# Regrouping small matmuls by TensorE mode and reordering two DMA queues in a fused attention and MLP kernel

## The chip, the cores and the metric

The kernel runs on one core of a Trainium2 chip. The metric is the device time of one execution in microseconds. Besides the time of whole runs I use a finer measure, because differences of 0.2 us are at stake in 290: inside a trace, the time from the start of one matmul to that of another.

## The reference, cut to what matters

```python
kv  = np.einsum('bhsd,bhse->bhde', k, v)          # 8 batches, 8 heads, 576 rows, 64 columns
out = np.einsum('bhsd,bhde->bhse', q, kv)         # linear attention, no softmax
x   = out / rms(out) * g_norm                     # per head
xn  = (x - mean) / sqrt(var + 1e-6) * g_ln        # per row of 512
y   = x + relu(xn @ w_ch1) @ w_ch2                # 512 -> 2048 -> 512
```

## The kernel before

Work is cut into tiles of 128 rows. A batch has 576 rows: four full tiles and a remainder of 64 rows, and two batches' remainders share a tile ("remainder 1" holds those of batches 0 and 1, and so on). For a full tile, `o` is four matmuls of the full form, 128 rows by 128 columns; `kv` of a batch and the remainder's `o` use only 64 of TensorE's columns at a time, because their outputs go to one half of the PSUM partitions each:

```python
def kv_of(b):                                     # 40 matmuls, 128 rows x 64 columns
    kv_ps = ps_m.tile([128, HP, D], f32, tag="misc", name="kv_ps")
    ...
                nc.tensor.matmul(kv_ps[hh * D:hh * D + D, hp, :],
                                 lhsT=k_in[b % NB][:, h, j, :], rhs=v_in[b % NB][:, h, j, :], ...)
    nc.scalar.copy(kvp[:D, :, :D], kv_ps[:D])
    nc.scalar.copy(kvp[D:, :, D:], kv_ps[D:])
```

TensorE's stream is the two large products (`mm1`, line 413, and `mm2`, line 429 of this kernel). It is counted in slots: one slot is four matmuls of 512 columns, or the like, about 0.87 us. An agenda, `at(slot, ...)`, pushes everything else in between; batch b's `mm1` begins at slot 32 b. The parts of a tile are set by `plan_tile`: `o`, its square and the sum of squares at slot s; VectorE's `y`, `x` and `xc` two slots later; the variance four slots after that; the transpose of `xc` by DMA at `turn_at`.

```python
for b in range(3, B):
    s = 32 * b
    at(47 if b == 3 else s - 60, lambda b=b: load_batch(b, ...))   # k, v, q of b on GpSimd's queue
    d = -41 if b == 3 else -45
    at(s + d + (1 if b < 5 else 0), lambda b=b: kv_of(b))
    at(s + d + 1.7, lambda b=b: turn_q_dma(b))                     # VectorE copy, SyncE DMA transpose
    for j in range(J):
        o = s + d + (11 if b == 3 else 13) + 5 * j
        plan_tile(o, lambda b=b, j=j: main_tile(b, j), o + 6, False)
    if b % 2:
        plan_tile(s - 14, lambda b=b: rem_tile(b), s - 8, False)
```

SyncE's queue carries, in program order, the output stores, the transposes of q (3.1 us to issue) and those of x (1.3 us). GpSimd's queue carries the loads. Before batch b's loads it copies one element of the transposed q of batch b-1, and for batch 4 also one of batch 2's last transposed x: a gate.

## Time and profile before

| | before |
|---|---|
| time, median of 4 runs | 290.69 us (290.39 to 290.95) |
| span of the profiled run | 288.8 us |
| TensorE busy | 280.9 us, 97% |
| VectorE, ScalarE | 149.8 and 153.2 us |
| kv and remainder blocks that stand alone between large products | 11 |

The page's chain of waits, by engine, is the quickest way to see how much of the span isn't TensorE's own stream:

```profile
PE 85%; DMA 5%; DVE 5%; ACT 2%; issue 1%; SPq 1%; DVEq 0%; POOLq 0%
```

It follows back what released what, so the 5% of DMA (7.05 us of it, 2.4%, are the first load of v) and the 5% of VectorE need not be idle time of TensorE: the chain runs through what released an instruction, even where TensorE had other work until then. How little it really waits is only visible from the starts of its matmuls, as the prediction reads them.

### The profile page before, as it was taken

How to read it: one execution, taken by the hardware profiler on the slowest of the kernel's cores; microseconds unless marked ns; L12 is line 12 of the kernel's file. 1: busy time of each engine (PE TensorE's matmuls, PEld its weight loads, DVE VectorE, ACT ScalarE, POOL GpSimd, SP SyncE). 2: the span in 40 equal slices, each digit the busy share in tenths (PEclk: the TensorE clock that was granted, in tenths of full speed). 3: DMA queues.
4: the chain of work that ended last, by engine and by line, in shares of the span. 5: the costliest groups of instructions: out<-in, count | busy, mean ns of one | idle time of the engine just before them, and what ended most of it. 6: DMA issues, size and time to landing. Idle time of an engine off the chain costs nothing.

```text
span 288.8 us, 5753 instructions
## 1 busy us (share of the span) xinstructions
PE 280.9 (97%) x2295; PEld 157.9 (55%) x2295; DVE 149.8 (52%) x331; ACT 153.2 (53%) x333; POOL 41.0 (14%) x69
## 2 busy tenths in 40 slices
PE   7889999999999999999999999999999999999994
PEld 3579756995479644444444444444444444444444
DVE  5774119938897783764376935762578200220022
ACT  3477844985379733872288318921893066016400
POOL 8522510041005004100500032000000000000000
PEclk9999999999999999999999999999999999999999
DMA  7999999979788959996994189947203410230033
GB/s 214 199 206 205 198 190 195 214 112 193 138 173 101 194 108 157 202 159 120 157 217 68 39 152 219 155 84 149 56 18 64 101 36 0 48 81 19 0 73 75
DMA packets 67546, 36.76 MB, mean 127 GB/s; under 512 B 35516, under 2 KB 62524, under 8 KB 67520
## 3 DMA queue, kind: packets, MB, share of 16 engines
q0 software_dynamic: 28528, 17.76, 43.8%
q1 hardware_dynamic: 38480, 17.91, 31.2%
q10 hardware_dynamic: 512, 0.72, 0.7%
q8 instruction: 18, 0.29, 0.4%
q14 instruction: 8, 0.07, 0.1%
HBM read 36.71 MB, written 9.44 MB: 160 GB/s over the span
## 4 chain that ended last, share of the span: by engine, by line
PE 85%; DMA 5%; DVE 5%; ACT 2%; issue 1%; SPq 1%; DVEq 0%; POOLq 0%
PE p L413 41%; PE p L429 37%; PE o_ps L271 2%; DMA v_in<-in_v_dram 2%; DMA qt<-q_p 2%; PE kv_ps L246 2%; DMA xT_blk<-xc 1%; DVE ss L298 1%; ACT m L416 1%; DVE x_blk L322 1%; DVE y L303 1%; DVE o_sb L434 1%; PE p L198 1%; SPq L205 1%; ACT rms L308 0%
## 5 line engine op out<-in xcount | busy, mean ns | idle before, releaser
L413 PE MATMUL p<-xT_blk,w_sb 128*128 128x128 bf16 (+2 forms) x1024 | 131.6, 286 | 0.6 <-DMA xT_blk<-xc 0.2
L429 PE MATMUL p<-w_sb,m 128*128 128x512 bf16 (+2 forms) x608 | 129.1, 368 | 0.0
L416 ACT ACTIVATE m<-p 128x512 bf16<-128x512 f32 x144 | 85.2, 596 | 43.0 <-PE p L413 40.5
L413 PEld LDWEIGHTS <-w_sb 128*128 128x128 bf16 x1024 | 78.7, 98 | 44.9 <-issue 1.5
L429 PEld LDWEIGHTS <-m 128*128 128x128 bf16 x608 | 57.0, 98 | 62.0
L434 DVE SCALAR_TENSOR_TENSOR o_sb<-p,rstd,x_blk 128x512 f32<-128x512 f32 (+2 forms) x38 | 27.3, 720 | 52.2 <-PE p L429 41.2
L277 ACT ACTIVATE sq<-o_ps 128x512 f32<-128x512 f32 x35 | 20.9, 596 | 41.7 <-PE o_ps L271 41.7
L298 DVE TENSOR_REDUCE ss<-sq 128x8 f32<-128x512 f32 x35 | 23.7, 678 | 13.0 <-ACT sq L277 12.9
L340 ACT ACTIVATE dev<-x_blk,st_blk 128x512 f32<-128x512 f32 x36 | 25.7, 714 | 6.2 <-DVE st_blk L326 6.1
L332 DVE SCALAR_TENSOR_TENSOR xc<-x_blk,st_blk,g_ln_sb 128x512 bf16<-128x512 f32 x34 | 25.6, 752 | 1.2
L303 DVE TENSOR_TENSOR y<-o_ps,inv 128x512 f32<-128x512 f32 x33 | 22.8, 692 | 3.4 <-PE p L413 0.5
L322 DVE SCALAR_TENSOR_TENSOR x_blk<-y,g_norm_sb 128x512 f32<-128x512 f32 x33 | 22.8, 692 | 1.1
L315 DVE RECIPROCAL inv<-rms 128x8 f32<-128x8 f32 x36 | 7.2, 201 | 23.0 <-ACT rms L308 23.0
L422 DVE RECIPROCAL rstd<-rstd 128x4 f32<-128x4 f32 x9 | 1.6, 175 | 31.2 <-ACT rstd L421 31.1
L308 ACT ACTIVATE rms<-ss,eps_sb 128x8 f32<-128x8 f32 x36 | 10.7, 296 | 11.5 <-DVE ss L298 11.4
L98 POOL COPY gate<-qt 1x1 bf16<-1x1 bf16 x5 | 0.9, 177 | 106.4 <-DMA qt<-q_p 106.4
L271 PEld LDWEIGHTS <-qt 128*128 128x128 bf16 (+1 forms) x156 | 10.2, 100 | 8.1 <-issue 1.7
L271 PE MATMUL o_ps<-kv_pack,qt 128*128 128x128 bf16 (+1 forms) x156 | 13.7, 220 | 0.2
L198 PE MATMUL p<-fill_sb 128*128 128x512 bf16 x27 | 8.0, 448 | 1.2 <-DVE eps_sb L137 1.2
L340 ACT ACTIVATION_READ_ACCUMULATOR dev<-x_blk,st_blk 128x1 f32 x36 | 6.8, 189 | 0.0
L249 ACT CAST kv_pack<-kv_ps 64x256 bf16<-64x256 f32 x7 | 2.6, 366 | 7.7 <-PE kv_ps L246 7.7
L246 PEld LDWEIGHTS <-k_in 128*64 128x64 bf16 x280 | 5.0, 112 | 2.6 <-issue 2.5
(80 smaller groups left out, 110.5 us busy)
## 6 DMA issues: line engine op xcount, KB each, us to landing
out_dram<-o_sb SPq DMA_DIRECT2D x70, 128.0 KB, 2.4
w_sb<-in_moe_w_ch_dram POOLq DMA_DIRECT2D x8, 512.0 KB, 15.2
q_in<-in_q_dram POOLq DMA_DIRECT2D x7, 320.0 KB, 12.3
k_in<-in_k_dram POOLq DMA_DIRECT2D x7, 320.0 KB, 6.0
v_in<-in_v_dram POOLq DMA_DIRECT2D x7, 320.0 KB, 8.6
q_in<-in_q_dram POOLq DMA_DIRECT2D x8, 256.0 KB, 12.3
k_in<-in_k_dram POOLq DMA_DIRECT2D x7, 256.0 KB, 6.7
v_in<-in_v_dram POOLq DMA_DIRECT2D x7, 256.0 KB, 10.6
```

Source lines behind the costliest of these rows:

```text
L198: nc.tensor.matmul(p1, lhsT=fill_sb[:, :128], rhs=fill_sb, start=True, stop=True)
L271: nc.tensor.matmul(flat[rows, hp * 128:(hp + 1) * 128], lhsT=lhsT_of(hp), rhs=kvp[:, hp, :], start=True, stop=True)
L277: nc.scalar.activation(self.sq_t, self.o_ps, func=AF.Square)
L298: nc.vector.tensor_reduce(self.ss, self.sq_t, axis=AX.X, op=ALU.add)
L303: nc.vector.tensor_mul(self.y_t, self.o_ps, self.inv().to_broadcast([128, H, D]))
L322: nc.vector.scalar_tensor_tensor(x_blk[:, ts].rearrange("p (h d) -> p h d", h=H), in0=self.y_t, scalar=1.0, in1=g_norm_sb.to_broadcast([12 ...
L332: nc.vector.scalar_tensor_tensor(self.xc_t, in0=x_blk[:, self.ts], scalar=st[:, 1, self.ts:self.ts + 1], in1=g_ln_sb, op0=ALU.add, op1=ALU ...
L340: nc.scalar.activation(dev, x_blk[:, ts], func=AF.Square, bias=st[:, 1, ts:ts + 1], accum_out=st[:, 2, ts:ts + 1])
L413: nc.tensor.matmul(p1[:, i, :], lhsT=w1_sb[:, kk, de * 128:(de + 1) * 128], rhs=blk[2][:, kk, sl], start=(kk == 0), stop=(kk == nK - 1))
L416: nc.scalar.activation(m1[:, de0:de0 + per, sl], p1, func=AF.Relu)
L429: nc.tensor.matmul(p2[:, c0:c1], lhsT=m1s[b][:, de, ts * 128:(ts + 1) * 128], rhs=w2_sb[:, de, c0:c1], start=(de == 0), stop=(de == nDe - 1))
L434: nc.vector.scalar_tensor_tensor(o_sb[:, c0:c1], in0=p2[:, c0:c1], scalar=rstds[b][:, ts:ts + 1], in1=blks[b][0][:, ts, c0:c1], op0=ALU.mu ...
```

## The change

The intent: kv products and remainder tiles, which share one form of TensorE, should stand together (remainders 1, 3, 5 behind kv of 3, of 4, and of 6 and 7), and the three short waits of TensorE near 83, 110 and 112 us should go, by shifting what stands before what on VectorE, SyncE and GpSimd.

```diff
+    def kv_of(*bs):
+        kv_ps = ps_m.tile([128, len(bs), HP, D], f32, tag="misc", name="kv_ps")
...
-    def plan_tile(s, make, turn_at, on_pe):
+    def plan_tile(s, make, turn_at, on_pe, x_at=None):
...
-        at(s + 2, second)
-        at(s + 6, third)
+        at(x_at or s + 2, second)
+        at((x_at or s + 2) + 4, third)
...
-        nc.sync.dma_start(dsts[0][:, c0:c1], o_sb[:64, c0:c1])
-        (nc.scalar if both else nc.sync).dma_start(dsts[1][:, c0:c1], o_sb[64:, c0:c1])
+        first = nc.gpsimd if b == 1 and ts >= 2 else nc.sync
+        first.dma_start(dsts[0][:, c0:c1], o_sb[:64, c0:c1])
+        (nc.scalar if both else first).dma_start(dsts[1][:, c0:c1], o_sb[64:, c0:c1])
...
-    for j, s, tn in ((0, 45, 51), (1, 49, 55), (2, 53, 61), (3, 57.5, 64)):
+    for j, s, tn in ((0, 45, 51), (1, 49, 55), (2, 53, 61), (3, 57.5, 63)):
...
+    at(100, lambda: load_batches((("k", 5), ("v", 5), ("q", 5)), turned_q(4)))
+    at(132, lambda: load_batches((("q", 6), ("k", 6), ("v", 6), ("k", 7), ("v", 7)), turned_q(5)))
+    at(164, lambda: load_batches((("q", 7),), turned_q(6)))
+    at(115, lambda: kv_of(5))
+    for s, bs, rem, x_at, tn in ((56, (3,), 1, 64, 69), (85, (4,), 3, 88, 94),
+                                 (152, (6, 7), 5, 154, 160)):
+        at(s, lambda bs=bs: kv_of(*bs))
+        plan_tile(s + .1, lambda rem=rem: rem_tile(rem), tn, False, x_at)
+    plan_tile(210, lambda: rem_tile(7), 216, False)
+    for b, at_q, at_o, step in ((3, 56.05, 67, 4.3), (4, 86, 97, 4.75),
+                                *((b, 32 * b - 43.3, 32 * b - 32, 5) for b in range(5, B))):
+        at(at_q, lambda b=b: turn_q_dma(b))
```

(The lines of the old loop that this replaces stand in the section on the kernel before.)

More of the change, by code (lines that the diff above doesn't have):

```diff
@@ L94, in load, with load_batches @@
         nc.gpsimd.dma_start(dst[64:, h0:h1, :J], up(t, b, h0, h1))
-    def load_batch(b, *after):
+    def load_batches(what, *after):
         for element in after:
             nc.gpsimd.tensor_copy(gate, element)
-        load(k_in[b % NB], k, b)
-        load(v_in[b % NB], v, b)
-        load(q_in[b % NB], q, b)
+        tensors = {"k": (k_in, k), "v": (v_in, v), "q": (q_in, q)}
+        for name, b in what:
+            dst, src = tensors[name]
+            load(dst[b % NB], src, b)
     def load_w1(c):
@@ L237, in times_g @@
             del self.even, self.odd
-    def kv_of(b):
-        kv_ps = ps_m.tile([128, HP, D], f32, tag="misc", name="kv_ps")
-        kvp = held[b] = kv_pack[b % 4]
-        for hp in range(HP):
-            for j in range(JJ):
-                for hh in range(2):
-                    h = 2 * hp + hh
-                    nc.tensor.matmul(kv_ps[hh * D:hh * D + D, hp, :],
-                                     lhsT=k_in[b % NB][:, h, j, :], rhs=v_in[b % NB][:, h, j, :],
-                                     start=(j == 0), stop=(j == JJ - 1))
-        nc.scalar.copy(kvp[:D, :, :D], kv_ps[:D])
-        nc.scalar.copy(kvp[D:, :, D:], kv_ps[D:])
+    def kv_of(*bs):
+        kv_ps = ps_m.tile([128, len(bs), HP, D], f32, tag="misc", name="kv_ps")
+        for i, b in enumerate(bs):
+            for hp in range(HP):
+                for j in range(JJ):
+                    for hh in range(2):
+                        h = 2 * hp + hh
+                        nc.tensor.matmul(
+                            kv_ps[hh * D:hh * D + D, i, hp, :], lhsT=k_in[b % NB][:, h, j, :],
+                            rhs=v_in[b % NB][:, h, j, :], start=(j == 0), stop=(j == JJ - 1))
+        for i, b in enumerate(bs):
+            kvp = held[b] = kv_pack[b % 4]
+            nc.scalar.copy(kvp[:D, :, :D], kv_ps[:D, i])
+            nc.scalar.copy(kvp[D:, :, D:], kv_ps[D:, i])
     def new_block(n, bufs):
@@ L592, in next_loads @@
         nc.gpsimd.memset(v_in[0][64:, :, J], 0.0)
-        load_batch(2)
+        load_batches((("k", 2), ("v", 2), ("q", 2)))
     at(1, before_1)
@@ L627, with turned_q @@
     at(36.9, lambda: turn_q_dma(2))
-    for j, s, tn in ((0, 45, 51), (1, 49, 55), (2, 53, 61), (3, 57.5, 64)):
+    for j, s, tn in ((0, 45, 51), (1, 49, 55), (2, 53, 61), (3, 57.5, 63)):
         plan_tile(s, lambda j=j: main_tile(2, j), tn, False)
-    plan_tile(62, lambda: rem_tile(1), 69, False)
     at(78, lambda: rstd_of(2))
-    for b in range(3, B):
-        s = 32 * b
-        at(47 if b == 3 else s - 60,
-           lambda b=b: load_batch(b, qts[b - 1][:1, J, HP - 1, 127:],
-                                  *([blks[2][2][:1, nK - 1, 511:]] if b == 4 else [])))
-        d = -41 if b == 3 else -45
-        at(s + d + (1 if b < 5 else 0), lambda b=b: kv_of(b))
-        at(s + d + 1.7, lambda b=b: turn_q_dma(b))
+    def turned_q(b):
+        return qts[b][:1, J, HP - 1, 127:]
+    at(47, lambda: load_batches((("k", 3), ("v", 3), ("q", 3)), turned_q(2)))
+    at(68, lambda: load_batches((("k", 4), ("v", 4), ("q", 4)),
+                                turned_q(3), blks[2][2][:1, nK - 1, 511:]))
+    at(100, lambda: load_batches((("k", 5), ("v", 5), ("q", 5)), turned_q(4)))
+    at(132, lambda: load_batches((("q", 6), ("k", 6), ("v", 6), ("k", 7), ("v", 7)),
+                                 turned_q(5)))
+    at(164, lambda: load_batches((("q", 7),), turned_q(6)))
[8 more added lines that the diff above has]
+        at(at_q, lambda b=b: turn_q_dma(b))
         for j in range(J):
-            o = s + d + (11 if b == 3 else 13) + 5 * j
+            o = at_o + step * j
             plan_tile(o, lambda b=b, j=j: main_tile(b, j), o + 6, False)
-        if b % 2:
-            plan_tile(s - 14, lambda b=b: rem_tile(b), s - 8, False)
-        at(s + 14, lambda b=b: rstd_of(b))
+        at(32 * b + 14, lambda b=b: rstd_of(b))
     at(32 * B + 14, lambda: rstd_of("rem"))
```

## The prediction

> **What bounds the kernel now.** I read the page first, then the chain of waits, then the order of time of TensorE alone, then that of the SyncE queue and of GpSimd. The page says who the bound is:
>
> ```profile
> PE 280.9 (97%) x2295; PEld 157.9 (55%) x2295; DVE 149.8 (52%) x331; ACT 153.2 (53%) x333; POOL 41.0 (14%) x69
> PEclk9999999999999999999999999999999999999999
> ```
>
> TensorE is busy 97% of the 288.8 us span at full clock, all others about half. A busy TensorE only says that matmuls were in flight, so I worked from starts: the time from the first matmul of a group to the first of the next, against the count times the undisturbed spacing. That spacing is read where nothing interferes: 64 matmuls of 128x512 from 243.39 to 257.21 us give 215.8 ns each, 40 of 128x256 from 83.34 to 87.71 give 109.1 ns, 48 of 128x128 from 62.68 to 65.36 give 55.8 ns. From 33 us on nearly every group runs at exactly these spacings. What is left over is of two kinds.
>
> The first is a toll around the kv products (line 246) and the remainder tiles (line 271, the form with 64 active columns). TensorE in order of time (start, duration, engine, line, what), batch 5's stretch:
>
> ```profile
> 156.11 1.89 PE L429 MATMUL p<-w_sb,m 128*128 128x512 bf16 x8
> 157.93 0.41 PE L271 MATMUL o_ps<-kv_pack,qt 128*64 128x128 bf16 x8
> 158.28 1.04 PE L429 MATMUL p<-w_sb,m 128*128 128x512 bf16 x4
> 159.24 0.82 PE L246 MATMUL kv_ps<-v_in,k_in 128*64 128x64 bf16 x40
> 160.00 11.40 PE L429 MATMUL p<-w_sb,m 128*128 128x512 bf16 x52
> ```
>
> From 156.11 to 157.93 eight matmuls took 1.82 us instead of 1.73: 94 ns lost on entering the 128*64 form. Four from 158.28 to 159.24 took 0.96 instead of 0.86: the same 94 ns before kv. On leaving, the last matmul of kv starts 129 ns before its successor where its own kind is spaced about 19 on average: 110 ns lost; after a remainder tile 133. This repeats at all seven kv blocks and all four remainder tiles (entry 93 to 117 ns, exit 109 to 133).
>
> The second kind is three waits:
>
> ```profile
> 81.15 1.91 PE L413 MATMUL p<-xT_blk,w_sb 128*128 128x256 bf16 x16
> 83.11 0.40 PE L271 MATMUL o_ps<-kv_pack,qt 128*128 128x128 bf16 x4
> ...
> 109.63 1.89 PE L429 MATMUL p<-w_sb,m 128*128 128x512 bf16 x8
> 111.63 0.40 PE L271 MATMUL o_ps<-kv_pack,qt 128*128 128x128 bf16 x4
> 112.25 4.48 PE L413 MATMUL p<-xT_blk,w_sb 128*128 128x512 bf16 x20 [0.23 <-DMA xT_blk<-xc]
> ```
>
> 81.15 to 83.11 is 1.96 us for 1.75 of work: 0.21 lost. 109.63 to 111.63 is 2.00 for 1.73: 0.27. 111.63 to 112.25 is 0.62 for 0.22: 0.39. Sum 0.87 us. The first two are o of batch 3's and batch 4's first tile waiting for the transposed q; the third is batch 3's first hidden matmul waiting for its last transposed x. The SyncE queue shows why:
>
> ```profile
> 103.73 0.59 SPq L448 DMA_DIRECT2D out_dram<-o_sb  x1
> 106.53 3.10 SPq L205 DMA_TRANSPOSE qt<-q_p  x1
> 109.69 1.26 SPq L352 DMA_TRANSPOSE xT_blk<-xc  x1
> 111.04 0.54 SPq L447 DMA_DIRECT2D out_dram<-o_sb  x1
> ```
>
> The x transpose at 109.69 had its input (xc, 102.5 us on VectorE) seven microseconds before, but stands behind the q transpose, which itself waited for VectorE's copy of q (105.65 to 106.47).
>
> **What the Trainium skill says.** "TensorEngine Tiling (Array Packing)", Key Properties: changing the tiling mode, not just the tile, drains TensorE. kv and remainder tiles both use 128 rows by 64 columns, everything around them 128 by 128; the trace agrees: 94 in, 110 to 133 ns out, and nothing at the ordinary o tiles (4 x 55.8 ns). "TensorE: Matmul & The Clock Gate", Back-to-back issue gap, puts the isolated 512-column gap at N/2.4 + 2.5 ns, about 216; the trace has 215.8. "DMA: Bandwidth & Descriptors", Issuing engines are not separate DMA queues: issuing from another engine saves only the sequencer's time to issue. Here that is the point of moving stores: SyncE spends 0.47 to 0.60 us on each and, in order, waits for its data.
>
> **The change part by part.** Slots are groups of four 128x512 matmuls (0.863 us) or the like.
>
> (a) Remainder tiles 1, 3, 5 directly behind kv of 3, 4, and of 6 and 7, and those two kv together. Removed: four times one exit and one entry, 0.110 + 0.094 = 0.204 us each, as long as kv to remainder is no mode change. 4 x 0.204 = 0.82 us, all on TensorE's own stream, so all on the path. Work added: none; the matmuls are the same in number and form.
>
> (b) First wait. q of batch 3 is still issued at about 78.1 us and lands at 83.06. Its first o moves from slot 66 to 67, one later (0.87 us), while TensorE comes 0.20 us earlier by (a): wanted at 83.1 - 0.21 - 0.20 + 0.87 = 83.56. Margin 0.5 us; the 0.21 goes.
>
> (c) Third and second wait. In the new order the last x transpose of batch 3 stands before q of batch 4 on the SyncE queue. VectorE per tile is one reduction, reciprocal, y, x and xc, 3.8 to 4.2 us a tile from the trace, so the closer tile step (4.3 slots, 3.97 us with the o) keeps it just fed: last xc at about 101.5, transposed and landed (2.5 us after issue) by about 106.5, wanted at 110.7. q of batch 4: VectorE copy at about 102.8, behind the reduction of remainder 3 only, since its y, x and xc moved to slot 88; queue free at 104.6, landed five us later (78.09 to 83.06 in this trace) at 109.6. Its o moved to slot 97, about 111.5. Margin 1.9 us. The 0.27 and 0.39 go.
>
> (d) Batch 1's last stores on GpSimd: four issues of 0.7 us (its loads' duration) at 82.6 to 86, before its gate for batch 4's load, which passed at 88.36. With SyncE free of them and the x transpose a slot earlier, that gate should pass near 86.5. It ends no wait by itself; it makes room for (c).
>
> (e) Loads of 6 and 7: five tensors in one go, then q of 7. In the trace three tensors took 13.1 us from first packet to last (140.4 to 153.6), with GpSimd's gate passing at 138.5. Shifted 1.2 us, two more at 3.6 us each in the nearly empty time after: the end is estimated at 159.5. kv of 6 and 7 in slot 152 would start at 161.8. Margin about 2 us, the thinnest new dependence with (b).
>
> Sum: 0.82 + 0.87 = 1.69 us. 290.94 - 1.69 = **289.25**. I add 0.15 for a small wait that I don't see: **289.4 us**.
>
> **The rivals.** First, a new wait takes the old ones' place: kv of 7 waits for v of 7. Batch 5's three tensors took 16.0 us, not 13.1; at that pace five end at 165, and 3 us are lost: about 292. For it: DMA is the one resource near full in bursts. Against it: from 154 to 160 us the queues carried almost nothing. I give a wait over 0.3 us there 15%. Second, the waits shift rather than vanish: VectorE falls behind in 70 to 100 us, because the tiles come closer and remainder 1's reduction now stands before the last tile of batch 2, or o waits for one of its two PSUM buffers, since remainder 1's o is held from slot 56 to 64. Either would keep 0.3 to 0.6 us: about 289.8. For it: the per-tile time of 3.8 to 4.2 us against a step of 3.97. Against it: four us of margin at the last x. 25%. Third, the toll belongs to each block and not to the change of mode, so that nothing is saved by neighbours: 290.1. Against it: the ordinary o tiles pay none. 10%.
>
> **Range and chances.** Main path 289.25; the rivals pull upward, to 289.8, 290.1, rarely 292; three runs of before spread over 0.56 us. Range 288.7 to 290.7. Two per cent is 5.8 us: more than all idle time on TensorE after 20 us, so faster is 1%; slower needs a wait of 6 us nobody hides, 1%; within 2% is 98%.
>
> **What would show it.** In the new trace TensorE should show line 246 directly followed by line 271 in three places, a single 80-matmul kv, one entry of about 94 ns and one exit of about 133 there; at 83, 110 and 111 us no group should exceed its count times its spacing by more than 0.05 us; SyncE should issue the last x of batch 3 before q of batch 4; GpSimd's load for batch 4 should start near 87 us. The span should be about 287.1. I am wrong if a gap over 0.3 us stands inside the kv of 6 and 7, if o of batch 3's first tile still waits, or if 90 ns appear between kv and remainder.

## The result, and the profile after

| | before | after |
|---|---|---|
| median of 4 runs | 290.69 us | 288.72 us (288.63 to 288.75) |
| span of the profiled run | 288.8 us | 286.7 us |
| ratio of the fast runs | | 0.9932, 95% interval 0.9915 to 0.9949 |

A ratio here is the mean time of one kernel's fast runs over that of the other's of the same rounds, so not quite the ratio of the medians. The gain is 0.7%, inside the range foretold. The page after, its chain by engine:

```profile
PE 91%; DMA 2%; DVE 2%; ACT 2%; issue 1%; DVEq 0%; POOLq 0%
```

SyncE has gone from the chain and DMA and VectorE have shrunk: what ended last is TensorE's own stream more than before. TensorE in order of time, the stretch of batch 4's second product (columns: start us, duration us, engine, line, what, how many):

```profile
154.71 7.07 PE L432 MATMUL p<-w_sb,m 128*128 128x512 bf16 x31
161.71 1.46 PE L247 MATMUL kv_ps<-v_in,k_in 128*64 128x64 bf16 x80
163.00 0.39 PE L274 MATMUL o_ps<-kv_pack,qt 128*64 128x128 bf16 x8
163.32 7.08 PE L432 MATMUL p<-w_sb,m 128*128 128x512 bf16 x31
170.24 0.39 PE L274 MATMUL o_ps<-kv_pack,qt 128*128 128x128 bf16 x4
```

80 matmuls of kv and 8 of remainder 5 stand together. This trace lacks 26 of the 2295 matmul records, one in each of the two 31s here (they are 32 and 32), but all the starts stand. 161.71 less 154.71 is 7.00 us, 32 spacings of 0.2158 are 6.90: one entry of 0.095. From 161.71 to 163.00 are 1.29 us, two kv of 0.644 with nothing between; the last matmul of kv starts 28 ns before the first of the remainder, where alone it starts 128 ns before its successor. The remainder takes 0.325 us with the exit, where alone it took 0.347, so a little is saved by starting behind kv too.

The three waits are gone. TensorE near 83 and near 111 us:

```profile
80.86 2.78 PE L416 MATMUL p<-xT_blk,w_sb 128*128 128x256 bf16 x24
83.48 0.39 PE L274 MATMUL o_ps<-kv_pack,qt 128*128 128x128 bf16 x4
...
110.62 1.03 PE L416 MATMUL p<-xT_blk,w_sb 128*128 128x512 bf16 x4
111.49 0.39 PE L274 MATMUL o_ps<-kv_pack,qt 128*128 128x128 bf16 x4
```

80.86 to 83.48 is 2.62 us, 24 spacings of 0.1091 are 2.62. 110.62 to 111.49 is 0.87 for 0.86. The SyncE queue in order of time after:

```profile
102.26 1.31 SPq L453 DMA_DIRECT2D out_dram<-o_sb  x1
103.62 1.29 SPq L355 DMA_TRANSPOSE xT_blk<-xc  x1
105.02 3.03 SPq L206 DMA_TRANSPOSE qt<-q_p  x1
108.16 0.54 SPq L452 DMA_DIRECT2D out_dram<-o_sb  x1
```

The x transpose now stands before the q transpose, and q is issued at 105.02 instead of 106.53.

The whole difference of the two spans, 288.83 less 286.72 = 2.11 us, splits at two matmuls that both traces have, the first of kv of batch 2 (slot 36) and the last of all:

| stretch | before | after | less by |
|---|---|---|---|
| start to kv of 2 | 53.20 | 53.14 | 0.06 |
| kv of 2 to last matmul | 231.66 | 229.87 | 1.79 |
| last matmul to end | 3.97 | 3.72 | 0.26 |

The middle stretch is the one that the change touches on TensorE. Its 1.79 us are four joined pairs of 0.224 (0.90, next section) and the three waits of 0.87; 0.02 remain. The first line is start-up, which varies from trace to trace: kv of 2 starts at 53.05 to 53.56 us in thirteen of the fourteen, at 54.93 in f1. The last was not foreseen, and is taken up below.

### The profile page after: what moved, and what is told of

Same layout as the page of the kernel before. It is cut to its first block, busy times and chain, and to the rows that moved or that the text cites. A ratio compares the mean times of both kernels' runs of the same rounds, so it can differ in the third digit from the quotient of the medians.

```text
span 286.7 us, 5727 instructions
## 1 busy us (share of the span) xinstructions
PE 277.8 (97%) x2269; PEld 158.0 (55%) x2295; DVE 150.0 (52%) x331; ACT 152.9 (53%) x333; POOL 43.1 (15%) x73
## 4 chain that ended last, share of the span: by engine, by line
PE 91%; DMA 2%; DVE 2%; ACT 2%; issue 1%; DVEq 0%; POOLq 0%
PE p L432 43%; PE p L416 42%; PE o_ps L274 3%; DMA v_in<-in_v_dram 2%; PE kv_ps L247 2%; ACT m L419 1%; DVE x_blk L292 0%; DVE xc L552 0%; ACT xT_blk L353 0%; PE tp L351 0%; ACT rms L311 0%; PE odd L226 0%; DVE ss L518 0%; PE tp L559 0%; DVE ss L301 0%
## 5 line engine op out<-in xcount | busy, mean ns | idle before, releaser
L432 PE MATMUL p<-w_sb,m 128*128 128x512 bf16 (+2 forms) x592 | 126.2, 368 | 1.2 <-issue 0.5
```

Source lines behind the costliest of these rows:

```text
L432: nc.tensor.matmul(p2[:, c0:c1], lhsT=m1s[b][:, de, ts * 128:(ts + 1) * 128], rhs=w2_sb[:, de, c0:c1], start=(de == 0), stop=(de == nDe - 1))
```

## The experiments

All were built on the changed kernel, most with one part altered (e5, e9, f1 and f2 alter several), and were run beside the kernel before: e1, e2, e3 and e6 on one chip, the others on another. The kernel before has a median of 290.45 to 290.58 us in these jobs. "Stretch" is kv of 2 to the last matmul in the run's trace; the changed kernel has 229.87 us, and 229.91 in a second profile (the control at the end).

| label | median us | lowest to highest | stretch us | against 229.87 |
|---|---|---|---|---|
| e1_rem_apart | 289.46 | 289.35 to 290.04 | 230.54 | +0.67 |
| e2_kv7_apart | 289.14 | 289.02 to 289.17 | 230.09 | +0.22 |
| e3_kv5_halves | 289.19 | 288.80 to 289.41 | 230.09 | +0.22 |
| e6_o3_slot66 | 289.54 | 289.24 to 289.61 | 230.46 | +0.59 |
| e7_q4_first | 289.36 | 288.66 to 289.43 | 230.59 | +0.72 |
| e8_rem3_x_early | 289.47 | 289.30 to 290.13 | 230.31 | +0.44 |
| e9_both | 291.36 | 291.11 to 292.24 | 232.01 | +2.15 |
| e4_sync_stores | 290.25 | 288.76 to 291.42 | 230.48 | +0.61 |
| e5_sync_stores_turn64 | 291.46 | 290.97 to 292.82 | 231.88 | +2.01 |
| c_changed_again | 288.89 | 288.64 to 290.05 | 229.91 | +0.04 |
| f1_rem7_joined | 290.90 | 290.22 to 292.36 | 231.70 | +1.83 |
| f2_two_clusters | 295.29 | 293.21 to 296.37 | 234.19 | +4.33 |

### The price of a change of mode

```diff
-        plan_tile(s + .1, lambda rem=rem: rem_tile(rem), tn, False, x_at)
+        plan_tile(s + 1, lambda rem=rem: rem_tile(rem), tn, False, x_at)
```

> Remainder tiles 1, 3 and 5 stand one slot behind their kv instead of directly behind it; all else as in the changed kernel. Mode theory (each change between the 128x64 and the 128x128 form of TensorE costs about 0.09 to 0.13 us): three more exits and entries, each about 0.22 us as the two traces show it, so +0.67 us against the changed kernel (about 289.4 us), and TensorE starts that show 94 ns before and 133 ns after each remainder tile again. Rival (the toll belongs to each block, and the whole gain came from the waits that the reordering ended): within 0.1 us of the changed kernel's 288.7.

The stretch grew by 0.674 us, 0.225 for each of three pairs, and the median run by 0.7. TensorE in order of time, remainder 1 one slot behind kv of 3 (the records behind it are left out):

```profile
72.65 0.82 PE L247 MATMUL kv_ps<-v_in,k_in 128*64 128x64 bf16 x40
73.40 1.04 PE L432 MATMUL p<-w_sb,m 128*128 128x512 bf16 x4
```

kv is back at 0.75 us to the next start (0.654 in the changed kernel), and the four matmuls behind it run to the remainder at 74.37, 0.97 us for 0.86: exit and entry are both paid.

```diff
-                                 (152, (6, 7), 5, 154, 160)):
+                                 (152, (6,), 5, 154, 160)):
+    at(156, lambda: kv_of(7))
```

> kv of 7 stands alone in slot 156 instead of in front of remainder 5 together with kv of 6. Mode theory: one more entry and exit, +0.20 to 0.22 us (about 288.9). Rival (that kv pair waits for its loads in the changed kernel, which a later slot would end): a gain of up to 0.3 us. Block rival: no difference.

+0.225 us, as the mode theory says. The rival that the pair was waiting for its loads falls: 80 matmuls in 1.29 us left no room for a wait, and the later slot gained nothing.

```diff
-    at(115, lambda: kv_of(5))
+    at(115, lambda: kv_half(5, 0, 2))    # the same matmuls, hp 0 and 1
+    at(116, lambda: kv_half(5, 2, 4))    # hp 2 and 3, then the copies
```

> The kv of batch 5 is cut into two halves of 20 matmuls in slots 115 and 116: the same 40 matmuls, one mode change in and out more. Mode theory: +0.20 us, 94 ns before and 110 ns after each half. Block rival (toll per product, spread over its matmuls): nothing, since each half has half the matmuls.

+0.224 us where 0.20 was expected, with the same matmuls in number and form. TensorE in order of time:

```profile
128.35 0.51 PE L250 MATMUL kv_ps<-v_in,k_in 128*64 128x64 bf16 x20
128.79 1.04 PE L451 MATMUL p<-w_sb,m 128*128 128x512 bf16 x4
129.76 0.51 PE L250 MATMUL kv_ps<-v_in,k_in 128*64 128x64 bf16 x20
```

Each half takes 0.44 us to the next start; twice 0.44 is 0.88 where the whole took 0.75, one exit more, and the 0.97 us of the four between them hold the second entry, 0.1. The toll is one per entry and exit, not per matmul. This is the cleanest test of the mode theory, since nothing was moved but the second half, by one slot.

### The first wait

```diff
-    for b, at_q, at_o, step in ((3, 56.05, 67, 4.3), (4, 86, 97, 4.75),
+    for b, at_q, at_o, step in ((3, 56.05, 66, 4.3), (4, 86, 97, 4.75),
```

> The four o tiles of batch 3 begin at slot 66 as in the kernel before instead of 67, step 4.3 kept. My account of the first wait (q of batch 3 lands at about 83.0 us whatever TensorE does; slot 66 comes at 82.6 now): TensorE waits 0.4 us at that o tile, total about +0.4 us (289.1). Rival (the first wait was ended by something else, the stores moved to GpSimd say): no wait, no difference.

```profile
81.11 1.91 PE L416 MATMUL p<-xT_blk,w_sb 128*128 128x256 bf16 x16
83.43 0.40 PE L274 MATMUL o_ps<-kv_pack,qt 128*128 128x128 bf16 x4 [0.42 <-DMA qt<-q_p]
```

81.11 to 83.43 is 2.32 us for 1.75: a wait of 0.58, named by the trace as q's transpose. One slot of delay ended the first wait, and the stores on GpSimd alone don't. My 0.4 was small: the slot came at 82.86 us, 0.25 later than I had taken it, like all of this run, but q landed 0.38 later than I had taken it.

### The second and third wait: three edits crossed

```diff
# e7: q of 4 turned right behind kv of 4
-    ... (4, 86, 97, 4.75), ...
+    ... (4, 85.05, 97, 4.75), ...
# e8: remainder 3's y, x, xc in slot 85
-    ... (85, (4,), 3, 88, 94), ...
+    ... (85, (4,), 3, 85.5, 94), ...
# e9: both (q at 85.6, still behind those and before the x transpose)
```

> q of batch 4 is turned right behind kv of 4, so that it stands before batch 3's last x on the SyncE queue, as in the kernel before; remainder 3's y, x and xc stay at slot 88. Order theory (the third wait was ended because the x transpose now stands before q): about +0.4 us, a wait before batch 3's first hidden matmul. VectorE theory (both waits were ended because remainder 3's y, x and xc no longer stand before VectorE's copy of q): q is issued near 103.6, x at 106.7 and lands near 109.3, wanted at 110.6: no wait, within 0.1 us of the changed kernel.

> Remainder 3's y, x and xc stand in slot 85 before VectorE's copy of batch 4's q, as in the kernel before; the x transpose still stands before q on the SyncE queue. VectorE theory: the copy comes near 106 to 107 us, q lands near 112, wanted at 111.5, and the output of batch 2's second tile frees its PSUM buffer late: about +0.5 us in one or both places. Order theory: no third wait, so at most +0.1 us.

> Both of the last two edits: remainder 3's y, x and xc before VectorE's copy of q, and q before batch 3's last x on the SyncE queue. VectorE theory with the queue behind it: q issued near 107, x at 110.1, landed near 112.7, wanted at 110.6: about +2.1 us (290.8), far more than the sum of the two edits alone (0 and 0.5). If the two add up, +0.5 to 0.9.

e8 came as VectorE's theory says: the copy stood behind the remainder's chain, at 106.07 us instead of 103.00, and its 0.44 us appeared at the PSUM buffer that VectorE frees with the output of batch 2's second tile. q landed just as its o tile came, after that shift, so without the wait for the buffer, one for q would have taken its place. e8, VectorE and then TensorE in order of time:

```profile
106.07 0.82 DVE L204 COPY q_p<-q_in 128x2560 bf16<-128x2560 bf16 x1
```

```profile
107.60 3.61 PE L432 MATMUL p<-w_sb,m 128*128 128x512 bf16 x16 [0.28 <-DVE o_sb L437]
```

e9 gave +2.15 against 2.1 worked out beforehand. TensorE in order of time, e9:

```profile
107.72 3.61 PE L432 MATMUL p<-w_sb,m 128*128 128x512 bf16 x16 [0.28 <-DVE o_sb L437]
112.88 1.02 PE L416 MATMUL p<-xT_blk,w_sb 128*128 128x512 bf16 x4 [1.54 <-DMA xT_blk<-xc]
```

16 matmuls from 107.72 end at 111.17, the next starts at 112.88: 1.71 us of waiting for the x transpose behind q, and 0.45 before it for the buffer. Together the two edits cost far more than the sum of 0.72 and 0.44, what each cost alone.

e7 went against both theories: +0.72 in the profiled run. VectorE in order of time shows a third cause:

```profile
104.69 0.83 DVE L204 COPY q_p<-q_in 128x2560 bf16<-128x2560 bf16 x1 [3.00 <-DMA q_in<-in_q_dram]
```

VectorE stood idle for 3.00 us for the load of q of batch 4, whose last packet came at 104.2 us in this run and at 101.8 in the first trace of the changed kernel. The copy was late for a new reason, and the x transpose behind it on SyncE with it. One of the four runs of e7, at 288.66, shows no loss, as one would have with the faster load; the other three are near 289.4. The control run of the changed kernel is the fairer comparison: there q of batch 4 landed just as late (104.36 us by its semaphore, 104.67 in e7), VectorE waited for it too, and the stretch lost 0.04 us, since the x transpose stood before it. So neither theory alone is right. The third wait takes a late copy of q and the order q before x together; what makes the copy late may be VectorE's work (before, e9) or the load (e7). The changed order takes x out of that line, and then the copy's lateness only matters to q itself. The later slot of batch 4's first o tile (96 to 97) was not undone in any run. In the first trace of the changed kernel q landed at 109.89 us and slot 96 came at 110.62, so there the slot wasn't needed.

### The stores on GpSimd

```diff
-        first = nc.gpsimd if b == 1 and ts >= 2 else nc.sync
+        first = nc.sync
```

> Batch 1's last two tiles are stored by SyncE again; batch 2's last x stays turned at slot 63. My estimate: SyncE issues the two x transposes near 83.8 and 85.1, the later lands near 87.8, wanted at 88.3; GpSimd's gate for batch 4 about 0.9 us later than in the changed kernel, hidden: within 0.1 us of it. Rival (the stores on GpSimd are what ends the waits): +0.4 us or more.

This expectation failed; the rival's size came, but in a wait that the rival doesn't name. TensorE in order of time:

```profile
96.14 4.48 PE L432 MATMUL p<-w_sb,m 128*128 128x512 bf16 x20
101.17 0.82 PE L247 MATMUL kv_ps<-v_in,k_in 128*64 128x64 bf16 x40 [0.54 <-DMA v_in<-in_v_dram]
```

kv of 4 waits for v of 4. GpSimd in order of time says when the load was issued, in e4:

```profile
87.99 0.18 POOL L98 COPY gate<-xT_blk 1x1 bf16<-1x1 bf16 x1 [4.28 <-DMA xT_blk<-xc]
89.18 0.68 POOL L93 DMA_DIRECT2D k_in<-in_k_dram  x1 [1.01 <-PE p L416]
```

and in the changed kernel:

```profile
86.90 0.18 POOL L98 COPY gate<-xT_blk 1x1 bf16<-1x1 bf16 x1 [1.84 <-DMA xT_blk<-xc]
88.22 0.71 POOL L93 DMA_DIRECT2D k_in<-in_k_dram  x1 [1.14 <-PE o_ps L274]
```

With SyncE busy with two of the stores, batch 2's last x transposes are issued later, the gate opens 1.1 us later and the load of batch 4 begins 1.0 us later. I had called this hidden. Whether it is depends on the load's own time as well: the runs of e4 go from 288.76, no loss at all, to 291.42. The kernel before shows that the later gate alone doesn't make the wait: its load began later still, at 89.54 us, v of 4 landed at 99.69 (landings here and below are read from the trace's semaphore records; no view prints them), and kv of 4 began at 100.23 without a wait. From the first issue of k to the landing of v it took 10.2 us there, 11.9 in e4, 9.8 in e5 below, and 10.4 and 11.8 in the two traces of the changed kernel. In the slower of the latter, the control, kv of 4 shows 0.04 us more than its toll. So the gate gives the load about one microsecond of room, and a slow load uses it up; in e4 both came together, and no run parts them.

```diff
-        first = nc.gpsimd if b == 1 and ts >= 2 else nc.sync
+        first = nc.sync
-    for j, s, tn in (... (3, 57.5, 63)):
+    for j, s, tn in (... (3, 57.5, 64)):
```

> Batch 1's last two tiles stored by SyncE and batch 2's last x turned at slot 64, so behind those stores, as in the kernel before. With the stores on SyncE alone the x transposes were issued at 84.0 to 86.6 us, GpSimd's gate passed at 88.0 and TensorE waited 0.54 us at kv of 4 for v. Queue theory: the last x is now issued 1.2 us later and lands near 89.3, wanted at 88.4: a wait of up to 0.9 us there, and the load of batch 4 starts 1.2 us later, so kv of 4 waits near 1 us more: +1.0 to 2.5 us against the changed kernel. If the wait at kv of 4 was only a slow load and not the later gate: as with the stores alone, +0 to 0.6.

+2.01 us, within what was foretold, but in one place and not two. SyncE in order of time, then TensorE:

```profile
85.42 0.54 SPq L452 DMA_DIRECT2D out_dram<-o_sb  x1
86.00 0.59 SPq L453 DMA_DIRECT2D out_dram<-o_sb  x1
86.64 4.76 SPq L355 DMA_TRANSPOSE xT_blk<-xc  x3
```

```profile
87.82 1.04 PE L416 MATMUL p<-xT_blk,w_sb 128*128 128x256 bf16 x8
90.69 2.79 PE L416 MATMUL p<-xT_blk,w_sb 128*128 128x256 bf16 x24 [1.84 <-DMA xT_blk<-xc]
```

Behind the last tile's stores the x transpose is issued at 86.64 (the first of the three that the row merges), and batch 2's second half of `mm1` waits for it from 88.69 (87.82 and 8 times 0.109) to 90.69. Issue to landing was 4.0 us, where I had reckoned 2.6; the same transpose took 4.1 us in the first trace of the changed kernel (issued 82.65) and 2.5 in e4, and why no run tells. At 2.6 us the wait would have been about 0.6, by my estimate from these numbers, so the longer landing makes some 1.4 of the 2.0, and that the sum was hit is luck. kv of 4, two microseconds later too, no longer waits. With neither part the stretch is 0.22 us longer than that of the kernel before, so the new tile order then costs more than it gains. x turned a slot sooner is enough to end the wait for x (e4); the stores on GpSimd with x at slot 64 were not run.

### The end of the kernel

The 0.26 us after the last matmul were a riddle of the first comparison. The traces show what goes with it: the time from the last matmul's start to the end is 3.97, 3.98 and 3.97 us in the three kernels that store batch 1's last two tiles from SyncE (before, e4, e5) and 3.72 to 3.75 in the ten others. Since e4 puts back these four stores and nothing else, the stores are the cause. At the end SyncE runs nine instructions in turn that wait for semaphores. Their starts, in us after the last matmul's start, from my reading of the trace's records of SyncE's semaphore instructions (no view prints them):

```
before   1.15 1.52 | 2.70 2.76 2.82 2.88 2.95 3.00 3.07
e4       1.15 1.53 | 2.71 2.77 2.84 2.89 2.96 3.02 3.08
after    1.15 1.22 1.28 1.34 1.85 1.91 | 2.70 2.76 2.82
control  1.15 1.22 1.28 1.34 1.84 1.90 | 2.71 2.77 2.83
```

The last landing comes at 2.70 us in all. Where the bar stands, SyncE has waited for it; each wait that stands behind it costs another 0.06 us, seven starts to 3.07 in one case and three to 2.82 in the other. Which semaphore the last store carries evidently changes with the number of stores before it on SyncE: four fewer there, and the last to land comes later in the row. That the stores do it is shown by e4; that they do it by way of the semaphores' numbers is inferred from the pattern over thirteen kernels.

### Control, and two attempts to go further

> The changed kernel unchanged, as a control beside the two joined versions: 288.7 us, up to 289.3 in runs in which the first load of batch 1 or the load of batch 4 comes late, since those landed up to 0.5 us and 2.4 us apart in the traces of the other runs.

288.89, six runs from 288.64 to 290.05: as expected, but for one run above 289.3. The ratio to before in this job was 0.9948 (0.9926 to 0.9970).

If a pair is worth 0.22 us, remainder 7, still alone, should join too:

```diff
-                                 (152, (6, 7), 5, 154, 160)):
+                                 (154, (6, 7), 5, 155.5, 162)):
-    plan_tile(210, lambda: rem_tile(7), 216, False)
+    plan_tile(154.2, lambda: rem_tile(7), 164, False, 157.5)
# q, k, v of 6 loaded behind those of 5; q of 6 and 7 turned at slots 134.5 and 145.9
```

> Remainder 7 joins kv of 6 and 7 and remainder 5 in slot 154; for it q of 6 and 7 are turned earlier (slots 134 and 146) and k, v, q of 6 are loaded right behind those of 5. Mode theory: one entry and one exit less, -0.22 us against the changed kernel (288.5). Rivals: the larger load delays batch 5's or 6's q (a wait before their o tiles), or four VectorE chains in a row hold a PSUM buffer: no gain or a loss of up to 1 us.

It lost 1.83 us in the trace and 2.0 in the median against the control. TensorE in order of time:

```profile
167.03 0.39 PE L274 MATMUL o_ps<-kv_pack,qt 128*64 128x128 bf16 x8
168.03 0.22 PE L274 MATMUL o_ps<-kv_pack,qt 128*64 128x128 bf16 x1 [0.61 <-ACT kv_pack L253]
168.80 0.38 PE L274 MATMUL o_ps<-kv_pack,qt 128*64 128x128 bf16 x7 [0.55 <-ACT kv_pack L253]
```

I had overlooked that remainder 7 multiplies by kv of 6 and 7 themselves, and these must first be copied out of PSUM by ScalarE, in four copies of 0.37 us. Remainders 1, 3 and 5 use kv of batches 0 and 1, 2 and 3, 4 and 5, all earlier than the kv in front of them, so nothing stands between. About 1.5 us were lost there and 0.5 at 142 us, before batch 5's first o tile and its successor.

> As the last, and kv of 5 joins kv of 4 and remainder 3 in slot 95, k and v of 5 being loaded behind those of 4 (q of 4 first). Mode theory: -0.44 us against the changed kernel (288.3). Rivals: the longer load of batch 4 delays the q transpose, or k and v of 5 are not there at slot 95: a wait of 0.5 to several us at 100 to 112 us.

f2 adds to this that k and v of 5 are loaded behind those of 4, and their kv joined in slot 95. It lost 4.3 us in the trace, which is that of the fastest of its six runs, and 6.4 in the median against the control: kv of 5 waited for v of 5 (2.6 us by the trace's own account), and the loss at remainder 7 came on top. Neither version beats the changed kernel. One with kv of 7 in a PSUM tile of its own, first in the group and copied during kv of 6, is untried.

## Why the prediction was right

**What bounds it, and the toll (a).** Right in kind. e1, e2 and e3 measure it independently: 0.225, 0.225 and 0.224 us a pair, where I had 0.204. The term was undersized by a tenth, because I had read the exit too small. In e3 the two halves take 0.876 us to their next starts, the whole 0.754: 0.122 for an exit where I had 0.110, for the 19 ns that I took off as kv's own spacing are a mean with the exit in it; without it they are 16. The four matmuls between the halves take 0.967 us for 0.863: 0.104 where I had 0.094, since the matmuls behind an exit run some 10 ns longer in all. In e1 a part of the same sum stands at the remainder, which alone takes 0.02 us longer than behind a kv. Four pairs are 0.90 instead of 0.82. The page "TensorEngine Tiling (Array Packing)", Key Properties, speaks of a drain on a change of mode and not of a tile; kv to remainder, a change of tile in one mode, indeed showed no gap over 28 ns. That a drain is what the time goes into no trace shows; it shows that the time goes with the change of form. The 215.8 ns that the prediction sets beside the isolated gap were read in a stream of 64 matmuls; for a sustained stream the same section, "TensorE: Matmul & The Clock Gate", Back-to-back issue gap, gives about 131 ns, which this trace does not bear out.

**The first wait (b).** Right: the delay by a slot did it, as e6 shows by taking it back. The margin was thinner than told, about 0.4 us (q landed at 83.12, the tile began at 83.48).

**The second and third (c).** The waits went; their sum was right but for 0.01 us (0.62 less 0.22 is 0.40, not 0.39). q issued at 105.02 against 104.6 foretold, its gate at 110.01 against a landing at 109.6, the o tile at 111.49 against 111.5. That the moved chain of remainder 3 matters is shown by e8 and e9. That the order on SyncE alone, undone, would cost nothing was an expectation of VectorE's theory in e7, and it fell, because the load of q can come late.

**The stores (d).** This step failed in one sentence: that they end no wait by themselves. The gate came at 86.90, against 86.5 foretold, and the load behind it at 88.22, not near 87. The step left the load of batch 4 out of the path, but v of 4 can land just when it is wanted, so the microsecond gained there is room against a slow load: with the stores back on SyncE e4 lost 0.61 us in the profiled run, where both came together. And the stores on GpSimd shortened the end of the kernel by 0.26 us, which nothing in the prediction looked at.

**The loads (e).** Right: the last packet of the five tensors came at 159.2 us against 159.5 foretold, and kv of 6 and 7 began at 161.71 against 161.8.

**The rivals.** None came. kv of 7 didn't wait for v, o of batch 3 didn't wait for its PSUM buffer, and the toll was one of mode and not of blocks. The 0.15 us that I had added for a wait that I didn't see was not needed.

**The number.** 289.4 foretold, 288.72 measured, inside the range by 0.02 us. The mechanisms held, but that the number did so too is partly luck: the base of 290.94 was 0.25 us above the median of 290.69 that four runs gave, 0.15 was added for nothing, and the gain was larger than counted. The difference against the kernel before is 1.97 us between medians instead of 1.54. In the two traces it is 2.11: 0.10 of the 1.79 us of the middle stretch I had not counted, 0.06 are start-up, and 0.26 the end of the kernel, which I had not looked at.

## What to carry to other kernels

Small products that use TensorE in another form than their surroundings cost a fixed toll per visit, here 0.22 us for entry and exit, for blocks of 20 and of 40 matmuls alike; let them share visits, as long as none needs the output of another through a copy. When an in-order queue carries both hurried and leisurely transfers, read what each item at its head is waiting for; a transfer that is ready and stands behind one that isn't waits for both. A slot of delay for the consumer can end a wait by itself (taking it back cost 0.59 us in e6), and margins against loads should be read over several runs, since one trace shows only one load.

## What the Trainium skill lacked or had wrong

- "TensorEngine Tiling (Array Packing)", Key Properties: it says that a change of tiling mode drains TensorE, without a cost. Here 94 ns on the way into 128x64, about 112 ns on the way out behind kv and 124 behind a remainder (128 and 152 ns from the last start to the next, less their own spacing of 16 and 28), some 10 ns more in the matmuls that follow, and 0.224 us for each visit saved.
- "DMA: Bandwidth & Descriptors", Issuing engines are not separate DMA queues: issuing from several engines saves only the sequencer's time to issue, "which is usually small relative to the DMA itself". The issues agree with that (0.47 to 0.60 us for a store, 2.6 us to its landing), but the section leaves out what the in-order queue does: SyncE waits at its head for data, and what is ready behind it waits too. In e5, four stores back on it and one transpose a slot later cost 2.0 us, about 0.6 of it by the later issue and the rest by a longer landing that no run explains.
- No page that I read tells of the row of semaphore waits at a kernel's end: nine in turn, those with nothing left to wait for about 0.06 us apart, of which seven or three began at or after the last landing, 0.25 us between two kernels with the same last store.
